# Attention and two expert layers on one core: weights split in small pieces, four more tiles turned on TensorE, scatters of one expert unordered, surplus count moved ahead

## The chip, the cores and the metric

The kernel runs on one core of one Trainium2 chip. The time is the device time of one execution in microseconds (us); what counts is the median of the runs. Engines are named as in the profile: PE is TensorE's matmuls, PEld its weight loads, DVE VectorE, ACT ScalarE, POOL GpSimd, SP SyncE, which here issues DMAs.

## The reference

Three layers follow each other, on 4 x 768 = 3072 tokens of 384 numbers:

```
for t: state = alpha_t * state + k_t v_t^T ; y_t = q_t state        # 8 heads of 48
P = exp(x @ w_gate), 8 rounds of row and column scaling            # layer 1
out = sum_e P[:, e] * (relu(x @ w1[e]) @ w2[e])                    # all 8 experts, F = 1024
logits = x @ w_gate + log1p(exp(x @ w_noise)) * noise              # layer 2
top2 of logits, softmax weights of the two
out[rows of e] += weight * (relu(x[rows of e] @ w1[e]) @ w2[e])    # for each of 8 experts
```

All inputs and the output are float32.

## The kernel before

Every product of two float32 operands is made of three matmuls of 16-bit halves: hi x hi, hi x lo, lo x hi. So weights and activations are split into a hi and a lo half, a step that takes an ACT instruction (hi) and a DVE instruction (lo = value - hi).

**Weights.** An expert x (0 to 7 in layer 1, 8 to 15 in layer 2) has seven blocks: three row blocks of W1, 1024 wide, and four of W2. `w_load` brings one block from SP's queue into a staging tile `wst`, of which there are two. `w_split` makes its halves in `WT[x % 2]` with L145 on ACT and L147 on DVE, 1024 elements to an instruction for W1, 768 for W2. Experts 1 to 6 (`STR`) use a scheme of seven block products in place of eight; for them `w_sums` (L128 to L130, POOL) adds three combinations of W2's blocks, and the split of a W2 block is one of 192 and one of 1152.

**Layer 1.** For each expert and 512 tokens, `s1` makes four pairs of hidden blocks: 18 matmuls (L273) into two banks, evicted by ACT (L279, L280, L285, L291), DVE (L296, six instructions) and POOL (L292). Then `s2` (L307) makes the second product into long banks that DVE adds to acc with the weight P (L317). Expert 0, expert 7 and the end use the plain form `g1`/`g2` (L195, L199, L226, L236 to L244).

**Layer 2.** A gate and a routing chain (ACT and DVE, L713 to L803) find each token's two experts. It reads tokens turned by SP (`xf`, L696) from x, which L688 on ACT and L689 on DVE write; SP writes x out to `xd` (L690). Each expert has 832 slots, seven tiles of 128 (the last 64), done in units of tiles 0 to 2 and 3 to 6. L813, L817 and the index matmul L824 find the slots' tokens; `gather` (L851, POOL) fetches a slot tile's rows; `xpose` turns it through `turn`, by a DMA transpose on SP (L696), or on PE with an ACT copy (L700, L701) for expert 0's first three tiles. `g1b` is the first product (L867, evicted by L870 on ACT and L871 on DVE), `g2b` the second (L226, L879 on DVE); L880 on POOL adds its rows to the output by an indirect DMA, a scatter. Behind everything `overflow` counts slots that found no place, from L893 to L906, reads the count into a register (L918) and runs a loop over them (L919), which with these inputs has no round.

**Order.** All instructions stand in each queue as the program emits them. Matmul functions call `pump(t)`, which moves an emission clock by an estimate of PE's time and lets side chains emit what is due. `w_pump` takes a step of the weight queue at most every 6.0 units of that clock, or 2.2 once all of layer 1's experts have their place; a step loads block i, sums block i-1 and splits block i-2. `w_need` takes all remaining steps when an expert is about to be used. The framework adds waits between instructions that touch the same memory; two scatters into the output count as such.

## Time and profile before

| | us |
|---|---|
| median of 3 runs | 2074.77 |
| lowest, highest | 2073.38, 2074.82 |
| the profiled execution | 2075.67 |
| its span, first to last instruction | 2073.9 |
| PE busy in it | 1984.0 |
| DVE, ACT, POOL busy | 1228.6, 671.5, 622.2 |

The profile is one execution taken by the hardware profiler; its times count from the first instruction. A timeline row gives the start, the length, the engine, the line, the operation with the tile written and the tiles read, the shape, and in brackets how long the engine idled before it and what released it. Rows of like instructions in a row are joined ("x3"). The names are those of the program's tiles: bank and long are accumulators of PE, wst the staging tile of weights, wt the split weights, hid the hidden activations, acc the sums of layer 1 and later slot tiles, ss the block sums.

### The profile page before, as it was taken

What the parts mean: (1) busy time and instruction counts of PE and PEld (TensorE: products, weight loads), DVE (VectorE), ACT (ScalarE), POOL (GpSimd) and SP (SyncE); (2) the same over time, 40 slices, a digit from 0 to 9 for tenths busy, and PEclk for the clock granted to TensorE, in tenths of its full rate; (3) what the DMA queues carried; (4) which work ended last, traced back from release to release, by engine and by line L of the source; (5) the groups of instructions that cost most, each with busy time, mean ns of one, the idle gap of its engine ahead of it and who ended that gap; (6) DMA issues with size and microseconds to landing.
All of it is one profiled execution on the core that took longest, in us unless ns stands there. A gap on an engine that the chain in (4) does not pass through costs nothing. (4 is left out here: it accounts for less than half of the span.)

```text
span 2073.9 us, 37502 instructions
## 1 busy us (share of the span) xinstructions
PE 1984.0 (96%) x15667; PEld 1332.4 (64%) x15667; DVE 1228.6 (59%) x2513; ACT 671.5 (32%) x1201; POOL 622.2 (30%) x452
## 2 busy tenths in 40 slices
PE   6999999999999999999999999999999889999996
PEld 5887656667667766776776677666555545555553
DVE  8889675765675576567557556554336645445431
ACT  5554422422342243234224323332222313222220
POOL 2433212422342352234225222321001234333322
PEclk9999999999999999999999999999999989999998
DMA  6333010100010010001001001003423448656631
GB/s 214 98 109 103 21 41 21 41 21 1 19 44 1 1 42 21 1 26 37 1 1 52 11 1 42 1 1 95 133 69 81 111 84 187 112 128 123 132 78 24
DMA packets 119580, 121.06 MB, mean 58 GB/s; under 512 B 68708, under 2 KB 101757, under 8 KB 119408
## 3 DMA queue, kind: packets, MB, share of 16 engines
q1 hardware_dynamic: 107984, 99.22, 17.2%
q0 software_dynamic: 11136, 18.89, 5.4%
q8 instruction: 124, 2.03, 0.4%
q10 hardware_dynamic: 288, 0.52, 0.1%
q14 instruction: 48, 0.39, 0.1%
HBM read 85.17 MB, written 21.63 MB: 51 GB/s over the span
## 5 line engine op out<-in xcount | busy, mean ns | idle before, releaser
L273 PE MATMUL bank<-xh,wt 128*128 128x512 f16 x1728 | 522.0, 380 | 6.3 <-DVE ss L296 3.8
L307 PE MATMUL long<-wt,hid 128*128 128x192 f16 x6048 | 508.8, 246 | 14.2 <-DVE acc L317 9.2
L292 POOL TENSOR_TENSOR hid<-ss,hid 128x1024 f16<-128x1024 f32 x144 | 307.0, 2132 | 705.6 <-ACT hid L291 651.3
L307 PEld LDWEIGHTS <-hid 128*128 128x128 f16 x6048 | 499.6, 98 | 27.1 <-issue 11.1
L273 PEld LDWEIGHTS <-wt 128*128 128x128 f16 x2592 | 253.1, 98 | 306.3 <-PE bank L273 6.1
L226 PE MATMUL bank<-wt,hid 128*128 128x384 f16 (+1 forms) x2496 | 422.4, 326 | 1.3 <-DVE hid L871 1.3
L226 PEld LDWEIGHTS <-hid 128*128 128x128 f16 (+1 forms) x2496 | 243.6, 99 | 162.6 <-issue 2.5
L273 PE MATMUL bank<-xl,wt 128*128 128x512 f16 x864 | 328.1, 380 | 0.0
L317 DVE SCALAR_TENSOR_TENSOR acc<-long,Pm,acc 128x192 f32<-128x192 f32 (+1 forms) x360 | 187.4, 534 | 169.8 <-PE long L307 167.5
L296 DVE SCALAR_TENSOR_TENSOR ss<-bank,ss 128x256 f32<-128x256 f32 x576 | 241.7, 421 | 58.2 <-ACT hid L285 39.6
L296 DVE SCALAR_TENSOR_TENSOR hid<-bank,hid 128x256 f16<-128x256 f32 (+1 forms) x288 | 159.1, 552 | 180.6 <-ACT ss L280 180.6
L291 ACT ACTIVATE hid<-ss 128x1024 f16<-128x1024 f32 x144 | 152.2, 1057 | 241.2 <-DVE ss L296 241.2
L147 DVE SCALAR_TENSOR_TENSOR wt<-wst,wt 128x1024 f16<-128x1024 f32 (+3 forms) x129 | 167.6, 1312 | 50.7 <-ACT wt L145 50.2
L867 PEld LDWEIGHTS <-wt 128*128 128x128 f16 x1152 | 112.3, 98 | 103.3 <-DMA xh<-acc 12.8
L279 ACT ACTIVATE hid<-bank 128x256 f16<-128x256 f32 x144 | 53.3, 370 | 382.9 <-PE bank L273 382.9
L880 POOL DMA_INDIRECT out_dram<-acc,ix x56 | 88.5, 1579 | 267.4 <-DVE acc L879 161.9
L870 ACT ACTIVATE hid<-bank 128x384 f16<-128x384 f32 (+1 forms) x128 | 65.4, 516 | 257.2 <-PE bank L867 255.9
L145 ACT ACTIVATE wt<-wst 128x1024 f16<-128x1024 f32 (+3 forms) x129 | 111.2, 882 | 94.9 <-DMA wst<-in_moe_w_dram 71.0
L871 DVE SCALAR_TENSOR_TENSOR hid<-bank,hid 128x384 f16<-128x384 f32 (+1 forms) x128 | 74.5, 589 | 106.0 <-ACT hid L870 106.0
L195 PE MATMUL bank<-xh,wt 128*128 128x512 f16 x384 | 121.8, 379 | 0.7 <-DVE acc L317 0.7
L867 PE MATMUL bank<-xh,wt 128*128 128x384 f16 (+1 forms) x576 | 107.6, 345 | 12.4 <-DMA xh<-acc 12.4
L285 ACT ACTIVATE hid<-bank 128x512 f16<-128x512 f32 x144 | 86.0, 597 | 66.3 <-PE bank L273 66.3
(187 smaller groups left out, 1655.1 us busy)
## 6 DMA issues: line engine op xcount, KB each, us to landing
wst<-in_moe_w_dram SPq DMA_DIRECT2D x45, 512.0 KB, 3.4
wst<-in_moe_w_dram SPq DMA_DIRECT2D x60, 384.0 KB, 3.2
la<-in_alpha_dram SPq DMA_DIRECT2D x24, 260.0 KB, 2.8
lk<-in_k_dram SPq DMA_DIRECT2D x24, 256.0 KB, 3.0
wt<-in_q_dram SPq DMA_DIRECT2D x22, 256.0 KB, 3.9
out_dram<-zero SPq DMA_DIRECT2D x6, 768.0 KB, 4.4
xd<-x SPq DMA_DIRECT2D x24, 192.0 KB, 1.9
wt<-in_v_dram SPq DMA_DIRECT2D x16, 192.0 KB, 4.1
```

What stands on the lines that cost most here:

```text
L145: nc.scalar.activation(t[:, o:o + n], src, AF.Copy, scale=SW)
L147: nc.vector.scalar_tensor_tensor(t[:, o + o1:o + o1 + n], src, SW, t[:, o:o + n], op0=OP.mult, op1=OP.subtract)
L195: nc.tensor.matmul(p, w1s(e, a, kc, f), x[:, kc, s], start=(n == 0), stop=(n == 3 * KC - 1))
L226: nc.tensor.matmul(p, h(a, f, s), w2s(x, b, f), start=(f + n == 0), stop=(f == FC - 1 and n == 2))
L273: nc.tensor.matmul(p, w1s(e, a, kc, f), x[:, kc, tok], start=(n == 0), stop=(n == 3 * KC - 1))
L291: nc.scalar.activation(lefts(e, nb, j, 0, S1, 4), sums, AF.Copy)
L292: nc.gpsimd.tensor_sub(lefts(e, nb, j, 1, S1, 4), sums, lefts(e, nb, j, 0, S1, 4))
L296: nc.vector.scalar_tensor_tensor(out, p, 0.0, x, op0=OP.max, op1=op)
L307: nc.tensor.matmul(out, left(e, nb, j, a, aop)[:, q * 128:(q + 1) * 128], w2t(e, b, wop, j), start=start and n == 0, stop=stop and n == 3 ...
L317: nc.vector.scalar_tensor_tensor(a, p, Pm[:, T, e:e + 1], a, op0=OP.mult, op1=OP.add)
L867: nc.tensor.matmul(p, w1s(x, a, kc, f), xt[:, b * KC + kc, :], start=(i == 0), stop=(i == 3 * KC - 1))
L880: nc.gpsimd.indirect_dma_start(out=out, out_offset=bass.IndirectOffsetOnAxis(ap=ix, axis=0), in_=y, in_offset=None, bounds_check=N - 1, oo ...
```

## The change

Four edits. First, `w_split`'s work is cut into pieces of at most 512 elements (W1) or 384 (W2), and `w_queue` becomes a generator: a step issues the hi of one piece and the lo of the piece before, with the next block's load at a block's first piece and the next block's `w_sums` at its third. The first step loads two blocks and issues the first hi at once. An expert of `STR` has 22 pieces, another 14, where there were 11 and 7. The spacing is 5.0 units for experts 2 to 6 and 2.2 for the others. Second, all seven slot tiles of expert 0 are turned on PE. Third, scatters of one expert are declared independent of each other; those of different experts still wait. Fourth, what `overflow` computed ahead of its read is emitted at unit 6 of layer 2, and only the read and the loop stay at the end.

```diff
--- before.py
+++ after.py
@@ -129,23 +129,35 @@
         g.tensor_sub(c[6], c[4], c[3])
         g.tensor_add(c[7], c[2], c[6])
 
-    def w_split(x, i, st):
-        t = W[x]
+    def w_pieces(x, i, st, most=1024):
+
         if i < KC:
-            todo = [(st[:, :F], i * F, F)]
+            todo = [(0, i * F, F)]
             o1 = W1N
         elif x in STR:
             o = 2 * W1N + (i - KC) * 7 * ND
-            todo = [(st[:, :ND], o, ND), (st[:, 2 * ND:8 * ND], o + ND, 6 * ND)]
+            todo = [(0, o, ND), (2 * ND, o + ND, 6 * ND)]
             o1 = W2N
         else:
-            todo = [(st[:, :2 * DM], 2 * W1N + (i - KC) * 2 * DM, 2 * DM)]
+            todo = [(0, 2 * W1N + (i - KC) * 2 * DM, 2 * DM)]
             o1 = FC * DM
-        for src, o, n in todo:
-            nc.scalar.activation(t[:, o:o + n], src, AF.Copy, scale=SW)
-        for src, o, n in todo:
-            nc.vector.scalar_tensor_tensor(t[:, o + o1:o + o1 + n], src, SW, t[:, o:o + n], op0=OP.mult,
-                                           op1=OP.subtract)
+        for c, o, n in todo:
+            m = n // -(-n // most)
+            for d in range(0, n, m):
+                yield st[:, c + d:c + d + m], W[x][:, o + d:o + d + m], W[x][:, o + o1 + d:o + o1 + d + m]
+
+    def w_hi(src, hi, lo):
+        nc.scalar.activation(hi, src, AF.Copy, scale=SW)
+
+    def w_lo(src, hi, lo):
+        nc.vector.scalar_tensor_tensor(lo, src, SW, hi, op0=OP.mult, op1=OP.subtract)
+
+    def w_split(x, i, st):
+        p = list(w_pieces(x, i, st))
+        for a in p:
+            w_hi(*a)
+        for a in p:
+            w_lo(*a)
 
     def w_alloc(x):
         W[x] = WT[x % 2]
@@ -844,6 +856,7 @@
 
     rng = {"r": 0, "y": 0}
     RW = {}
+    SC = {}
 
     def gather(e, j):
         r = M2["rows"][rng["r"] % len(M2["rows"])]
@@ -854,7 +867,7 @@
         RW[e, j] = r
 
     def xpose(e, j, dst):
-        turn(dst, RW.pop((e, j)), e == 0 and j < J0)
+        turn(dst, RW.pop((e, j)), e == 0)
 
     def g1b(x, par, f, xt, n):
         if f == 0:
@@ -877,11 +890,18 @@
         y = M2["ys"][rng["y"] % len(M2["ys"])][:n]
         rng["y"] += 1
         nc.vector.tensor_scalar(y, p, wc, None, op0=OP.mult)
-        nc.gpsimd.indirect_dma_start(out=out, out_offset=bass.IndirectOffsetOnAxis(ap=ix, axis=0), in_=y,
-                                     in_offset=None, bounds_check=N - 1, oob_is_err=False, compute_op=OP.add)
-
-
-    def overflow():
+        d = nc.gpsimd.indirect_dma_start(out=out, out_offset=bass.IndirectOffsetOnAxis(ap=ix, axis=0), in_=y,
+                                         in_offset=None, bounds_check=N - 1, oob_is_err=False, compute_op=OP.add)
+        if x < 2 * E:
+
+            for o in SC.setdefault(x, []):
+                tc.declare_no_dep(d.ins, o, reason="rows of one expert's slots are distinct")
+            SC[x].append(d.ins)
+
+
+    OV = {}
+
+    def overflow_count():
         V = nc.vector
         so = ctx.enter_context(tc.tile_pool(name="over", bufs=1))
 
@@ -915,6 +935,12 @@
         vs, vt = t("vs", [128, NT, 5], BF), t("vt", [128, E, NT, 5], BF)
         ri1, ri2 = t("ri1", [128, KC], I32), t("ri2", [128, FC], I32)
         xto = t("xto", [128, 2 * KC, 128], F16)
+        OV.update({k: v for k, v in locals().items() if k not in ("V",)})
+
+    def overflow():
+        V = nc.vector
+        t, tot, NO, it, sel, s2, eb, rb, cu, ce, ei, w1i, w2i, vs, vt, ri1, ri2, xto = [
+            OV[k] for k in "t tot NO it sel s2 eb rb cu ce ei w1i w2i vs vt ri1 ri2 xto".split()]
         nv = nc.values_load(tot[0:1, 0:1], min_val=0, max_val=E * NO)
         with tc.For_i(0, nv, 1):
             V.tensor_scalar(sel, ce, it, None, op0=OP.is_le)
@@ -969,7 +995,6 @@
 
     NB = N // 512
     NW = KC + 4
-    st_ = {}
     ws0 = [0]
 
     def w0_step():
@@ -1098,28 +1123,47 @@
     queued = set()
 
     def w_queue(x):
-        wq.append(lambda: w_alloc(x))
-        for i in range(NW + 2):
-            def f(i=i):
-                if i > 1:
-                    w_split(x, i - 2, st_.pop((x, i - 2)))
-                if 0 < i <= NW:
-                    w_sums(x, i - 1, st_[x, i - 1])
-                if i < NW:
-                    st_[x, i] = w_load(x, i)
-            wq.append(f)
+
+        def steps():
+            w_alloc(x)
+            st = [w_load(x, 0), w_load(x, 1)]
+            last = None
+            for i in range(NW):
+                p = list(w_pieces(x, i, st[i], 512 if i < KC else 384))
+                if x in STR and i == KC:
+                    w_sums(x, i, st[i])
+                    yield
+                for n, a in enumerate(p):
+                    w_hi(*a)
+                    if last is not None:
+                        w_lo(*last)
+                    if n == 0 and i and i + 1 < NW:
+                        st.append(w_load(x, i + 1))
+                    if n == 2:
+                        w_sums(x, i + 1, st[i + 1]) if i + 1 < NW else None
+                    last = a
+                    yield
+            w_lo(*last)
+
+        s = steps()
+
+        def step():
+            return next(s, 0) is None
+
+        wq.append(step)
 
     w_at = [0.0]
 
     def w_pump():
         if wq and clk[0] >= w_at[0]:
-            wq.pop(0)()
-            w_at[0] = clk[0] + (6.0 if len(W) < E else 2.2)
-
+            if not wq[0]():
+                wq.pop(0)
+            w_at[0] = clk[0] + (5.0 if 2 < len(W) < E else 2.2)
 
     def w_need(x):
         while x not in W or (wq and x == max(W)):
-            wq.pop(0)()
+            if not wq[0]():
+                wq.pop(0)
 
     def gates(Ts):
         c = []
@@ -1243,6 +1287,8 @@
         if m < len(order2):
             e, j0, j1 = order2[m]
             a = [(lambda f=f: u1(m, f), 9 * ((min(CAP, j1 * 128) - j0 * 128) / 2400.0 + 0.0025)) for f in range(FC)]
+            if m == 6:
+                chain([(overflow_count, 1.0)])
             if m >= 4 and j0 == 0:
                 chain(columns(e, J0, NJ) + (rows_in(e + 1, 0, NJ, NT, NJ) + columns(e + 1, 0, J0) if e + 1 < E else []))
         if m:
```

Where the order moves, first on DVE, in layer 1, at the end of a cycle of expert 2 while expert 3's weights are split. Before (L296 evicts s1's banks, L317 those of s2):

```order
L296 SCALAR_TENSOR_TENSOR hid<-bank,hid 128x256
L296 SCALAR_TENSOR_TENSOR ss<-bank,ss 128x256
L147 SCALAR_TENSOR_TENSOR wt_3694<-wst,wt_3694 128x192
L147 SCALAR_TENSOR_TENSOR wt_3694<-wst,wt_3694 128x1152
L296 SCALAR_TENSOR_TENSOR ss<-bank,ss 128x256 x3
L296 SCALAR_TENSOR_TENSOR hid<-bank,hid 128x512
L317 SCALAR_TENSOR_TENSOR acc<-long,Pm,acc 128x192
L317 SCALAR_TENSOR_TENSOR acc<-long,Pm,acc 128x384
L317 SCALAR_TENSOR_TENSOR acc<-long,Pm,acc 128x192
```

After (L153 is now the lo, L308 and L329 are what L296 and L317 were):

```order
L308 SCALAR_TENSOR_TENSOR hid<-bank,hid 128x512
L153 SCALAR_TENSOR_TENSOR wt_3694<-wst,wt_3694 128x512
L308 SCALAR_TENSOR_TENSOR hid<-bank,hid 128x256
L308 SCALAR_TENSOR_TENSOR ss<-bank,ss 128x256 x4
L308 SCALAR_TENSOR_TENSOR hid<-bank,hid 128x512
L308 SCALAR_TENSOR_TENSOR hid<-bank,hid 128x256
L308 SCALAR_TENSOR_TENSOR ss<-bank,ss 128x256
L153 SCALAR_TENSOR_TENSOR wt_3694<-wst,wt_3694 128x512
L308 SCALAR_TENSOR_TENSOR ss<-bank,ss 128x256 x3
L308 SCALAR_TENSOR_TENSOR hid<-bank,hid 128x512
L329 SCALAR_TENSOR_TENSOR acc<-long,Pm,acc 128x192
```

The pairs of 192 and 1152 elements are gone; single pieces stand between the evictions.

Next on ACT, at the flush ahead of expert 1 of layer 2, behind the routing's exponentials. Before (L145 is the hi, L760 the routing, L870 g1b's eviction):

```order
L145 ACTIVATE wt_3694<-wst 128x1024
L145 ACTIVATE wt_3694<-wst 128x768
L760 ACT_TABLE_LOAD
L760 ACTIVATE wb<-wb 128x10
L145 ACTIVATE wt_3694<-wst 128x768 x3
L870 ACTIVATE hid<-bank 128x384 x8
L870 ACTIVATE hid<-bank 128x448 x14
```

After (L150 is the hi, L772 the routing, L883 g1b's eviction, L713 the copy of a tile turned on PE):

```order
L150 ACTIVATE wt_3694<-wst 128x512
L150 ACTIVATE wt_3694<-wst 128x384
L772 ACT_TABLE_LOAD
L772 ACTIVATE wb<-wb 128x10
L150 ACTIVATE wt_3694<-wst 128x384 x7
L883 ACTIVATE hid<-bank 128x384 x8
L713 ACTIVATE xh<-bank 128x6x128 x3
L713 ACTIVATE xh<-bank 128x6x64
L883 ACTIVATE hid<-bank 128x448 x8
```

The five hi instructions of 1024 and 768 elements have become nine of 512 and 384, with the same evictions behind them, and four copies of turned tiles have come between the two units' evictions.

Last on POOL, the end of its queue, with the semaphores that an instruction waits for in brackets (DMASW are those of POOL's own DMAs). Before:

```order
L880 DMA out_dram<-acc,ix 3072x384 [waits DMASW4_49,DVE_49]
L880 DMA out_dram<-acc,ix 3072x384 [waits DMASW5_49,DVE_49]
L880 DMA out_dram<-acc,ix 3072x384 [waits DMASW6_49,DVE_49]
L893 IOTA oth 128x22
L908 IOTA ei 128x8
L910 IOTA w1i 128x3
L912 IOTA w2i 128x8
L918 TENSOR_LOAD tot [waits DVE_49]
```

After:

```order
L893 DMA out_dram<-acc,ix 3072x384 [waits DMASW4_49,DMASW5_49,DMASW3_49,DMASW6_49,DMASW2_49,DMASW7_49,DMASW0_49,DVE_49]
L893 DMA out_dram<-acc,ix 3072x384 [waits DVE_49] x6
L944 TENSOR_LOAD tot [waits DVE_49]
```

The last six scatters wait for DVE alone, only an expert's first waits for those before it, and nothing but the read stands behind them.

## Rows read from the trace of the kernel before

**Rows 1.** The page: busy time by engine; a load's issue to landing.

```profile
PE 1984.0 (96%) x15667; PEld 1332.4 (64%) x15667; DVE 1228.6 (59%) x2513; ACT 671.5 (32%) x1201; POOL 622.2 (30%) x452
...
wst<-in_moe_w_dram SPq DMA_DIRECT2D x45, 512.0 KB, 3.4
```

**Rows 2.** Timeline of weight loads in layer 1: starts of s2.

```profile
376.67 3.04 PEld L307 LDWEIGHTS <-hid 128*128 128x128 f16 x35
...
442.31 7.74 PEld L307 LDWEIGHTS <-hid 128*128 128x128 f16 x92
...
530.51 14.01 PEld L307 LDWEIGHTS <-hid 128*128 128x128 f16 x168
...
559.91 3.04 PEld L307 LDWEIGHTS <-hid 128*128 128x128 f16 x35
...
622.19 7.90 PEld L307 LDWEIGHTS <-hid 128*128 128x128 f16 x94
...
1279.50 2.05 PEld L307 LDWEIGHTS <-hid 128*128 128x128 f16 x23
...
1310.78 14.01 PEld L307 LDWEIGHTS <-hid 128*128 128x128 f16 x168
```

**Rows 3.** Timeline, expert 3's weights: DVE's pair, PE's two waits.

```profile
593.48 3.24 DVE L147 SCALAR_TENSOR_TENSOR wt<-wst,wt 128x192 f16<-128x192 f32 x2
...
594.50 3.23 PE L307 MATMUL long<-wt,hid 128*128 128x192 f16 x37 [0.41 <-POOL hid L292]
598.95 6.26 PE L307 MATMUL long<-wt,hid 128*128 128x192 f16 x74 [1.23 <-DVE acc L317]
```

**Rows 4.** Timeline of PE: three single waits.

```profile
310.78 0.38 PE L273 MATMUL bank<-xh,wt 128*128 128x512 f16 x1 [2.54 <-DVE acc L236]
...
1445.69 0.19 PE L713 MATMUL bank<-g,xf 128*128 128x32 f16 x1 [2.42 <-DMA xf<-x]
...
1733.66 0.76 PE L824 MATMUL bank<-rhs,acc 128*128 128x35 bf16 x24 [2.24 <-DVE rhs L817]
```

**Rows 5.** Timeline of SP, ACT and PE, first unit of layer 2.

```profile
1604.42 1.22 SPq L112 DMA_DIRECT2D wst<-in_moe_w_dram  x1
...
1606.31 0.49 ACT L870 ACTIVATE hid<-bank 128x384 f16<-128x384 f32 x1 [3.25 <-PE bank L867]
...
1616.94 0.19 PE L713 MATMUL bank<-g,xf 128*128 128x32 f16 x1 [1.59 <-DMA xf<-x]
```

**Rows 6.** Timeline of POOL, SP and PE: expert 0's tiles 3 to 6.

```profile
1655.56 1.56 POOL L880 DMA_INDIRECT out_dram<-acc,ix  x1 [3.84 <-issue]
...
1661.46 0.99 POOL L851 DMA_INDIRECT acc<-xd,ix  x1 [0.30 <-issue]
...
1660.94 5.68 SPq L696 DMA_TRANSPOSE xh<-acc  x4
...
1668.72 2.77 PE L867 MATMUL bank<-xh,wt 128*128 128x448 f16 x7 [12.43 <-DMA xh<-acc]
```

**Rows 7.** Timeline of DVE and POOL, the end.

```profile
2053.84 0.61 DVE L879 TENSOR_SCALAR acc<-bank,wc 64x384 f32<-64x384 f32 x1 [3.40 <-PE bank L226]
...
2060.05 1.42 POOL L880 DMA_INDIRECT out_dram<-acc,ix  x1 [3.40 <-DMA out_dram<-acc,ix]
...
2062.74 0.13 DVE L904 CAST tot<-cu 1x1 int32<-1x1 f32 x1
```

**Rows 8.** Timeline of DVE: lo halves while little else runs.

```profile
296.73 0.35 DVE L147 SCALAR_TENSOR_TENSOR wt<-wst,wt 128x192 f16<-128x192 f32 x1
297.42 1.36 DVE L147 SCALAR_TENSOR_TENSOR wt<-wst,wt 128x1152 f16<-128x1152 f32 x1 [0.35 <-ACT wt L145]
```

**Rows 9.** Timeline of ACT and DVE: flush ahead of layer 2's expert 1.

```profile
1634.17 0.84 ACT L145 ACTIVATE wt<-wst 128x768 f16<-128x768 f32 x1 [3.19 <-DMA wst<-in_moe_w_dram]
...
1635.16 0.95 DVE L147 SCALAR_TENSOR_TENSOR wt<-wst,wt 128x768 f16<-128x768 f32 x1
```

**Rows 10.** Busy time by window: PE, PEld, DVE, ACT, POOL; granted clock, DMA.

```profile
1734.00:2053.80 319.80, 319.80 (x1985) 186.59 (x1981) 143.35 (x311) 79.83 (x132) 102.26 (x77) 1.00 0.56 111
```

## The prediction

> **What bounds the kernel now.** I read the page's busy times first: PE works 96% of the span, DVE 59%, ACT 32%, POOL 30% [rows 1]. So time can be won only where PE stands still, or in what follows PE's last instruction, and work put on DVE, ACT or POOL costs nothing as long as PE does not wait for it. From there I followed PE's idle time in the timeline, stretch by stretch, and looked for what released each wait. Three kinds came out.
>
> First, in layer 1, PE alternates between s1 (L273) and s2 (L307) in cycles that can be measured from one s2 to the next, on the weight-load rows. An undisturbed cycle runs from 530.51 to 559.91: 29.40 us. While expert 3's weights are split, two cycles take 559.91 to 622.19, 62.28, which is 3.48 more than two undisturbed ones; experts 4, 5 and 6 repeat that pattern (four times 3.48 = 13.9). Expert 2's two cycles, 376.67 to 442.31, lose 65.64 - 58.80 = 6.84, and expert 7's one, 1279.50 to 1310.78, loses 1.88. Together **22.6 us** go in cycles in which weights are split [rows 2]. Why is seen on DVE: a pair of lo halves (192 and 1152 elements) holds it 3.24 us in one piece at 593.48, the evictions of s1's banks and s2's banks stand behind it, and PE then waits 0.41 for POOL's part of hid and 1.23 for DVE's acc [rows 3].
>
> Second, five single waits at the seams: 2.54 at the change of bank pools, 2.42 for a transposed token tile, 2.24 for the right-hand side of the index matmul [rows 4], and in the first experts of layer 2 one of 1.59 [rows 5] and one of 12.43 [rows 6].
>
> Third, the end: DVE evicts the last tile at 2053.84, but the last scatter is issued only at 2060.05, since each waits for the landing of the one before; the count of surplus slots comes after it, and its last result stands at 2062.74. From its end, 2062.87, to the span's end at 2073.9 lie 11.0 us of leaving the loop [rows 1, 7].
>
> **The change part by part.** The profiled execution took 2075.67 us; the sum is made against it. The median of three runs, 2074.77, is 0.9 lower, and I take that off at the end.
>
> *Small pieces in layer 1.* A lo piece has at most 512 elements and stands alone between two groups of evictions. Quiet rows give its price: 192 elements took 0.35, 1152 took 1.36 [rows 8], so 1.05 ns an element and 0.15 fixed, and 512 take 0.69. The pair at 593.48 took 3.24 where the quiet prices make 1.71, a factor of 1.9 [rows 3, 8], so a piece beside POOL's work takes up to 1.3. PE's two waits behind the pair come to 1.64, so that DVE could be held for 3.24 - 1.64 = 1.6 without harm [rows 3]; 1.3 is less. The steps of one expert are also spread wider: 23 at 5.0 units of the emission clock instead of 9 at 6.0. What may stay is POOL: w_sums is as long as before and still stands ahead of L292 in some blocks; one wait of 0.41 for it [rows 3] at each of five sums for some of the experts makes 2 to 4, of which I take 3. **-19.6**; bounds -13 (a third of the losses stays) and -22 (nearly all goes).
>
> *Expert 1 and the seam at 310.* Expert 1's splits now come more often, and early, so less of them stands in front of L236 at the pool change. A shorter DVE queue takes part of the 2.54 [rows 4], I take somewhat over half: **-1.5**, between 0 and -2.5.
>
> *The token tile at 1445.* Its transpose stands on SP's queue behind a weight load that waits for a staging buffer. With the lo of a smaller, earlier piece as the last reader, this buffer comes free sooner: **-2.0** of 2.42 [rows 4], between 0 and -2.4.
>
> *First experts of layer 2, three terms.* (a) The first hi piece is now issued on ACT right behind its own load. SP issues that load at 1604.42, and a 512 KB load takes 3.4 us to land [rows 1, 5], so ACT is blocked until about 1608.6, where it evicted at 1606.31 before. Queued behind are the first g1b evictions and the L688 copies, on which the xd writes and the xf transposes on SP depend, past a load that now waits for a lo piece of its own. PE's wait for xf, 1.59 [rows 5], grows by 2.3 plus half a microsecond of pieces: **+3.0** (2 to 4). (b) In the flush ahead of expert 1 the last weight load now waits for a lo piece that stands behind the routing chain r4 on DVE. Before, its hi started at 1634.17 and its lo at 1635.16, with r4 ahead of that; now a lo of 0.55, and then a landing of up to 3.4, follow on 1635.16, so that DVE's evictions behind all this start near 1639.1 instead of 1636.1: **+3.1** (0 to 4) [rows 1, 9]. (c) After its last g2b matmul PE waits 12.43 for expert 0's four slot tiles. POOL's scatter at 1655.56 waits 3.84 for the one before, the gathers stand behind it, and SP's four transposes start at 1660.94 with 5.68 us of issue [rows 6]. The fourth gather is issued at 1661.46; with a landing taken as long as a load's, 3.4, its tile is there at 1664.9, and six PE transposes and one ACT copy of 768 elements, as long as the 0.84 of another ACT row of 768, end near 1666.2 instead of PE's 1668.72: -2.5, without SP's row of four [rows 1, 6, 9]. And the scatter ahead need not wait, which brings the gathers forward by half of the 3.84, -1.9; the other half goes to DVE's eviction, which then sets this scatter. **-4.4** (-2 to -7). Together **+1.7**, bounds -5 and +6.
>
> *The index matmul at 1733.* Its right-hand side stood on DVE behind a lo that waited for a load. Fewer pieces now stand ahead: **-2.2** of 2.24 [rows 4], between 0 and -2.2.
>
> *The rest of layer 2.* From 1734 to 2053.8 PE is busy 319.80 of 319.80 us [rows 10]: here the change can only lose. Seven more pieces an expert cost DVE 7 x 0.15 = 1 us, hidden as it idles over half of the stretch. The blocking first hi costs ACT a landing, 3.4, behind the flush's last one, say 7 us in all. PE's cover is the banks: 319.80/1985 is 0.161 a matmul, nine matmuls fill a bank in 1.45, eight banks hold 11.6 us. **0**, up to +3.
>
> *The end.* The scatters of the last expert no longer wait for each other, so the last one follows DVE's 2053.84 + 0.61 at about 2054.8 instead of 2060.05, and no count follows: the read of the count starts near 2056.2 instead of 2062.9, and the 11.0 us behind stay [rows 7]. **-6.6**; -5 if the landing of the last scatter, which the exit waits for, comes after that, -7.5 at best.
>
> **Sum:** 2075.67 - 19.6 - 1.5 - 2.0 + 1.7 - 2.2 + 0 - 6.6 = 2045.5; less 0.9, 2044.6: **2045 us**.
>
> **The rivals.** *Pieces that still collide.* If each small piece meets POOL, half of layer 1's gain goes: of the 22 pieces for each of experts 2 to 6, 110 in all, a fifth that make PE wait 0.4 to 0.5, as it did for POOL's hid [rows 3], come to 10: 2055 us. For it: the pair's factor of 1.9; against: a piece leaves DVE free again behind it. Chance 0.16. [...]
>
> *Fixed cost of more instructions.* 11 more pieces for each of six experts cost DVE 66 x 0.15 = 9.9 us; were DVE the path there, the time would be 2055. DVE's 59% speaks against. Chance 0.05. [...] The trace shows 0.15 for the fixed part, and PE does not wait for it.
>
> *The end stays.* If the exit is bound by the queue's drain and not by the scatters, or the declared independence leaves the waits in place, the 6.6 stay: 2052. The instruction order shows these waits gone; the count is moved for certain. Chance 0.09.
>
> *Slower.* ACT's blocked first piece and the flush ahead of each layer-2 expert: beyond 11.6 us of blocked ACT, PE stops. To turn the sum over, it takes some 5 us for each of seven experts, so blocks of 16.6 us, five landings of 3.4 in a row: 2045 + 35 = 2080. Against: the old flush already holds such a row of pieces, with PE never waiting [rows 10]. Chance 0.06.
>
> **How the numbers follow.** Forecast 0.64 (2038 to 2051), rivals 0.16, 0.05, 0.09 and 0.06. The range **2037 to 2056** takes in the bounds of the terms and the first three rivals' times, and leaves out the slow end and the far sides. About 4 us, 0.2%, is what can be told from no change. Faster 0.91, within 0.2% 0.03, slower 0.06.
>
> **What would show it.** Cycles of 29.4 between s2's in experts 2 to 7, with no DVE row over 1.4 us among L153; PE's wait for xf near 4.5 and the wait for xh near 8; at the end each scatter right behind its eviction, and 11 us of leaving behind the read of the count. It is wrong if the cycles still show 1 us or more each, if PE waits in 1734 to 2050, or if the wait for xh stays at 12.

## The result

The changed kernel takes **2049.76 us**, median of four runs (2048.4 to 2050.4); the kernel before, in the same runs, 2074.39 (2073.38 to 2074.82). The ratio is 0.9876, with a 95% interval from 0.9862 to 0.9889: 24.6 us, or 1.2%, faster. The forecast was 2045, in a range from 2037 to 2056; the time lies inside, 4.8 above the forecast.

The two profiled executions, 2075.67 and 2048.4, differ by 27.3, since that of before is above its median and that of the changed kernel is the fastest of its four. What follows is read from these two, so its sums come to 27.2, the difference of the spans.

The page of the changed kernel (span, then busy time by engine), which answers to [rows 1]:

```profile
span 2046.7 us, 37798 instructions
...
PE 1984.3 (97%) x15691; PEld 1334.8 (65%) x15691; DVE 1247.3 (61%) x2642; ACT 681.5 (33%) x1334; POOL 602.7 (29%) x452
```

PE's busy time, in which its stretches at half clock (a granted clock of 0.50 or 0.51 in windows below) count too, is the same to 0.3 us. On balance, what was won is time in which PE stood still (21.2 us) or had ended (6.3); stretches at half clock went in some places and came in others.

Where s2 starts in layer 1, timeline of weight loads, while expert 3's weights are split; it answers to [rows 2]:

```profile
553.05 14.01 PEld L319 LDWEIGHTS <-hid 128*128 128x128 f16 x168
...
582.45 14.01 PEld L319 LDWEIGHTS <-hid 128*128 128x128 f16 x168
...
611.85 14.01 PEld L319 LDWEIGHTS <-hid 128*128 128x128 f16 x168
```

Twice 29.40, and one unbroken row of 168 loads in each: an undisturbed s2. All cycles of experts 3 to 6 read like this. Expert 2's lose 0.85, 0.52 and 1.16, expert 7's 1.80, where they lost 6.84 and 1.88.

PE's single waits, timeline, to be held against [rows 4 to 6]:

```profile
309.91 0.38 PE L285 MATMUL bank<-xh,wt 128*128 128x512 f16 x1 [1.63 <-DVE acc L248]
...
1597.25 0.21 PE L725 MATMUL bank<-g,xf 128*128 128x32 f16 x1 [4.48 <-DMA xf<-x]
1597.43 3.04 PE L880 MATMUL bank<-xh,wt 128*128 128x384 f16 x9
...
1628.48 0.66 PE L238 MATMUL bank<-wt,hid 128*128 128x384 f16 x3 [0.93 <-DVE hid L884]
1630.57 1.14 PE L238 MATMUL bank<-wt,hid 128*128 128x384 f16 x3 [1.43 <-DVE hid L884]
...
1646.83 0.51 PE L712 MATMUL bank<-i,acc 128*128 128x128 f16 x6 [2.57 <-DMA acc<-xd,ix]
...
1651.38 2.99 PE L880 MATMUL bank<-xh,wt 128*128 128x448 f16 x8 [0.64 <-ACT xh L713]
```

The waits for the token tile at 1445 and for the index matmul at 1733 have no row any more. The wait for xf has grown to 4.48, and the nine matmuls behind it take 3.04 where nine took 1.62 in the undisturbed piece ahead of it. The wait of 12.43 has become four short ones (2.57, 0.72, 0.39 and 0.64) with transposes between them. The end, timeline of DVE and POOL, answers to [rows 7]:

```profile
2032.97 0.61 DVE L892 TENSOR_SCALAR acc<-bank,wc 64x384 f32<-64x384 f32 x1 [3.40 <-PE bank L238]
...
2029.85 1.55 POOL L893 DMA_INDIRECT out_dram<-acc,ix  x1 [2.35 <-DVE acc L892]
2033.86 1.42 POOL L893 DMA_INDIRECT out_dram<-acc,ix  x1 [2.46 <-DVEq L945]
```

The last scatter stands 0.9 behind DVE's eviction instead of 6.2.

Cut at the same PE instructions, the two traces differ like this (before, after; starts of the named matmuls, in us):

| stretch | before | after | difference |
|---|---|---|---|
| up to the first s1 | 310.78 | 309.91 | -0.9 |
| layer 1's cycles of s1 and s2 | 1084.32 | 1064.25 | -20.1 |
| up to layer 2's first g1b | 209.55 | 207.91 | -1.6 |
| to the first matmul behind the wait for xf and its gate | 12.45 | 15.36 | +2.9 |
| to the second unit's g1b | 13.38 | 15.98 | +2.6 |
| to the end of g2b ahead of tiles 3 to 6 | 25.81 | 30.85 | +5.0 |
| to the g1b of tiles 3 to 6 | 12.43 | 7.12 | -5.3 |
| that unit and its g2b, to expert 1's second unit | 32.58 | 31.35 | -1.2 |
| to expert 2's first unit | 32.96 | 30.66 | -2.3 |
| from there to PE's last instruction | 319.54 | 319.54 | 0.0 |
| behind PE's last instruction | 20.06 | 13.74 | -6.3 |

### The profile page after: what moved, and what is told of

The parts are those of the page before. It is cut to its first block, busy times and chain, and to the rows that moved or that the text cites. A ratio compares the mean times of both kernels' runs of the same rounds, so it can differ in the third digit from the quotient of the medians.

```text
span 2046.7 us, 37798 instructions
## 1 busy us (share of the span) xinstructions
PE 1984.3 (97%) x15691; PEld 1334.8 (65%) x15691; DVE 1247.3 (61%) x2642; ACT 681.5 (33%) x1334; POOL 602.7 (29%) x452
## 5 line engine op out<-in xcount | busy, mean ns | idle before, releaser
L304 POOL TENSOR_TENSOR hid<-ss,hid 128x1024 f16<-128x1024 f32 x144 | 306.7, 2130 | 701.8 <-ACT hid L303 658.7
L329 DVE SCALAR_TENSOR_TENSOR acc<-long,Pm,acc 128x192 f32<-128x192 f32 (+1 forms) x360 | 187.5, 534 | 148.1 <-PE long L319 147.4
L308 DVE SCALAR_TENSOR_TENSOR hid<-bank,hid 128x256 f16<-128x256 f32 (+1 forms) x288 | 159.3, 553 | 185.8 <-ACT ss L292 185.8
L308 DVE SCALAR_TENSOR_TENSOR ss<-bank,ss 128x256 f32<-128x256 f32 x576 | 241.0, 421 | 48.0 <-ACT hid L297 31.2
L303 ACT ACTIVATE hid<-ss 128x1024 f16<-128x1024 f32 x144 | 152.2, 1057 | 231.8 <-DVE ss L308 231.8
L153 DVE SCALAR_TENSOR_TENSOR wt<-wst,wt 128x384 f16<-128x384 f32 (+2 forms) x258 | 200.8, 789 | 23.6 <-ACT wt L150 23.6
L291 ACT ACTIVATE hid<-bank 128x256 f16<-128x256 f32 x144 | 53.2, 369 | 409.1 <-PE bank L285 409.1
L150 ACT ACTIVATE wt<-wst 128x384 f16<-128x384 f32 (+2 forms) x258 | 132.1, 538 | 130.9 <-DMA wst<-in_moe_w_dram 130.7
L883 ACT ACTIVATE hid<-bank 128x384 f16<-128x384 f32 (+1 forms) x128 | 63.7, 515 | 167.0 <-PE bank L880 167.0
L880 PE MATMUL bank<-xl,wt 128*128 128x384 f16 (+1 forms) x576 | 105.3, 339 | 0.0
```

The costliest lines, as they stand in the source:

```text
L150: nc.scalar.activation(hi, src, AF.Copy, scale=SW)
L153: nc.vector.scalar_tensor_tensor(lo, src, SW, hi, op0=OP.mult, op1=OP.subtract)
L303: nc.scalar.activation(lefts(e, nb, j, 0, S1, 4), sums, AF.Copy)
L304: nc.gpsimd.tensor_sub(lefts(e, nb, j, 1, S1, 4), sums, lefts(e, nb, j, 0, S1, 4))
L308: nc.vector.scalar_tensor_tensor(out, p, 0.0, x, op0=OP.max, op1=op)
L329: nc.vector.scalar_tensor_tensor(a, p, Pm[:, T, e:e + 1], a, op0=OP.mult, op1=OP.add)
```

## Which edit gives what: each one alone

Four kernels hold one edit each. First the pieces:

```diff
-        turn(dst, RW.pop((e, j)), e == 0)
+        turn(dst, RW.pop((e, j)), e == 0 and j < J0)
-            for o in SC.setdefault(x, []):
-                tc.declare_no_dep(d.ins, o, ...)
...
-            if m == 6:
-                chain([(overflow_count, 1.0)])
...
+    overflow_count()
     overflow()
```

> The small pieces alone, with the slot tiles, the scatters and the count as before. Theory (PE's waits add up, stretch by stretch, and a short wait that makes the granted clock fall costs its slow matmuls too): as in the changed kernel, layer 1's cycles give 18.4 us, the seam at 310 2.6, the token tile at 1445 2.2 and the index matmul at 1733 2.2; the first experts of layer 2 lose 5.5 at PE's wait for xf (2.9 longer, 2.6 in matmuls at half clock) and 5 at the flush; the wait for expert 0's tiles stays near 12.4 and the end stays at 20 us behind PE. Sum about -15: 2059. Rival (the pieces carry the whole result, the three other edits nothing): 2050.

Measured: 2059.99 in four runs, ratio 0.9924 (0.9907 to 0.9941), so 15.2 less than the 2075.21 of its own runs of before, as summed. The cycles lose what they lose in the changed kernel, the first matmul behind the wait for xf comes late in the same way, and 19.7 us stand behind PE's last instruction. One row missed: the wait for xh is 10.45, where 12.4 was expected. The pieces do not carry the rest.

Then the turns on PE:

```diff
-        turn(dst, RW.pop((e, j)), e == 0 and j < J0)
+        turn(dst, RW.pop((e, j)), e == 0)
```

> The kernel before, with expert 0's tiles 3 to 6 turned on PE, nothing else. Theory: the four transposes leave SP, PE's wait for xh falls from 12.4 to about 10, its matmuls at half clock behind the wait stay; about -2.5: 2072. Rival (the gathers alone set that wait): the wait stays at 12 or more and the time within 1 us of before.

Measured: 2069.52 in one run; PE ends 5.55 earlier than in the trace of before. That is twice the expectation. The g1b of tiles 3 to 6 starts 3.5 earlier, and then the unit behind it takes 31.05 instead of 32.58. The timeline of PE and the windows (busy PE, PEld, DVE, ACT, POOL, then granted clock, DMA share, GB/s) show why:

```profile
1660.71 0.82 PE L700 MATMUL bank<-i,acc 128*128 128x128 f16 x6 [4.63 <-DMA acc<-xd,ix]
1661.94 0.82 PE L700 MATMUL bank<-i,acc 128*128 128x128 f16 x6 [0.41 <-DMA acc<-xd,ix]
1663.11 1.46 PE L700 MATMUL bank<-i,acc 128*128 128x128 f16 x12 [0.35 <-DMA acc<-xd,ix]
1665.21 13.08 PE L867 MATMUL bank<-xh,wt 128*128 128x448 f16 x63 [0.64 <-ACT xh L701]
```

```profile
1660.00:1666.00 6.00, 3.89 (x27) 2.76 (x28) 0.00 (x0) 2.81 (x4) 3.54 (x3) 0.54 0.46 92
1666.00:1669.00 3.00, 3.00 (x14) 1.40 (x13) 0.30 (x1) 0.54 (x1) 0.00 (x0) 0.79 0.07 12
1668.70:1674.00 5.30, 5.30 (x30) 2.74 (x29) 5.30 (x26) 1.63 (x3) 0.00 (x0) 1.00 0.01 3
```

In the trace of before the granted clock was 0.51 from 1668.7 to 1674, in matmuls of 448 columns:

```profile
1668.70:1674.00 5.30, 5.28 (x15) 2.19 (x16) 1.15 (x5) 0.55 (x1) 0.00 (x0) 0.51 0.00 0
```

Here part of the stretch at half clock passes while the short transposes run, and the matmuls are back at 1.00 from 1668.7 on. What this is worth is not sharp: the same unit took 31.57 with the pieces alone, without these transposes, and 31.35 with them in the changed kernel.

Then the scatters:

```diff
+            for o in SC.setdefault(x, []):
+                tc.declare_no_dep(d.ins, o, reason="rows of one expert's slots are distinct")
+            SC[x].append(d.ins)
```

> The kernel before, with scatters of one expert not ordered among each other, nothing else. Theory: the scatter ahead of expert 0's gathers goes out about 2 us sooner and PE's wait for xh falls from 12.4 to about 10.4; at the end the last scatter follows PE by 1 us instead of 6.3, the count still behind it, so 5.3 less: together -7, 2067. Rival (the exit is bound by the queue's landing and drain, not by the scatters' order): the end stays at 20 us behind PE, and only 2 are gained, 2072.

Measured: 2071.71 in ten runs, ratio 0.9979 (0.9969 to 0.9988): 3.5, half of what was expected. The two mechanisms are there in the profile, at their size: PE's wait for xh is 10.27, 2.2 shorter, and 14.7 us stand behind PE's last instruction, 5.3 less.

```profile
1668.09 12.19 PE L868 MATMUL bank<-xh,wt 128*128 128x448 f16 x54 [10.27 <-DMA xh<-acc]
```

```profile
2055.88 1.42 POOL L881 DMA_INDIRECT out_dram<-acc,ix  x1 [2.46 <-DVE acc L880]
```

1.2 goes back at once: the wait for the index matmul's right-hand side grows from 2.24 to 3.47, since PE gets there sooner and DVE does not. Another 1.2 goes behind that longer wait, where the matmuls run at a granted clock of 0.65 (1733.5 to 1738); in the trace of before it is 1.00 behind the wait of 2.24. The profiled execution also reached its first s1 1.9 later than that of before, ahead of everything that was changed (below).

Last the count:

```diff
+            if m == 6:
+                chain([(overflow_count, 1.0)])
```

> The kernel before, with the count of surplus slots emitted at unit 6 of layer 2, nothing else. Theory: the scatters are still in a row, the last one issued 6.2 us behind PE and landed 9 us behind it; the exit waits for that landing anyway, so the count's 2.9 us behind the scatter are worth at most 1.4: 2073 to 2074. Rival (the count is what sets the end): 2.9 gained or more, 2071.

Measured: 2073.88 in one run, 18.6 behind PE's last instruction, 1.5 less. From the end of the last scatter's instruction to the end of the span lie 12.39 in the four traces with the count behind it (before, the pieces, the turns, the scatters) and 11.3 to 11.4 without, so the count is worth about 1. That the exit waits for the scatter's landing, as expected, is not shown. One run, where before spreads from 2072.3 to 2080.4, shows no gain by its time. With both edits it is 13.7, so the scatters' order was most of the end.

## Size or density of the pieces

The prediction held that the length of one piece decides: 1.3 fits where 3.2 did not. Four kernels vary the length and the density of the steps. Large pieces, spread:

```diff
-                p = list(w_pieces(x, i, st[i], 512 if i < KC else 384))
+                p = list(w_pieces(x, i, st[i], 1024 if i < KC else 1152))
-                    if n == 2:
+                    if i >= KC and n == min(2, len(p) - 1):
-            w_at[0] = clk[0] + (5.0 if 2 < len(W) < E else 2.2)
+            w_at[0] = clk[0] + (10.0 if 2 < len(W) < E else 4.4 if len(W) <= E else 2.2)
```

> The changed kernel with pieces as large as before (1024; 192 and 1152; 768), the steps spread over as many cycles as in the changed kernel (10.0 units for experts 2 to 6, 4.4 for 1, 7 and 8). Theory (the length of one DVE instruction decides): pairs of 3.2 us between evictions still stop PE, layer 1's cycles lose 3 or more for each of experts 3 to 6 and some 15 to 22 in all. Rival (the spread decides, not the size): experts 3 to 6 lose less than 1 each, and layer 1 about 4 to 6 in all, as the changed kernel does.

Small pieces, dense:

```diff
-            w_at[0] = clk[0] + (5.0 if 2 < len(W) < E else 2.2)
+            w_at[0] = clk[0] + (2.6 if 2 < len(W) < E else 2.2)
```

> The changed kernel with its small pieces, issued twice as densely for experts 2 to 6 (2.6 units), so that an expert's weights take as many cycles as before. Theory (the length of one DVE instruction decides): experts 3 to 6 lose less than 1 each, layer 1 at most 10. Rival (the spread decides): they lose 2 to 3.5 each again, layer 1 some 15 to 20.

The kernel before, with its steps wider and nothing else:

```diff
-            w_at[0] = clk[0] + (6.0 if len(W) < E else 2.2)
+            w_at[0] = clk[0] + (12.0 if 2 < len(W) < E else 6.0 if len(W) < E else 2.2)
```

> The kernel before with one number changed: steps 12.0 units of the emission clock apart for experts 2 to 6, not 6.0; the pieces as large as they were, the pair of 192 and 1152 still in one step. Theory now (how much DVE and POOL work falls into one cycle decides, more than the length of a piece): layer 1's cycles lose 8 or less instead of 24.6 (1.9 of it ahead of expert 7, which no weights cause), so some 15 below before, 2059. Rival (a pair of 3.2 stops PE wherever it stands): the same number of pairs costs the same, 3 or more for each of experts 3 to 6, and the time stays within 4 of before.

Large single pieces, dense, against the first of these:

```diff
-            w_at[0] = clk[0] + (10.0 if 2 < len(W) < E else 4.4 if len(W) <= E else 2.2)
+            w_at[0] = clk[0] + (5.0 if 2 < len(W) < E else 4.4 if len(W) <= E else 2.2)
```

> The kernel with large single pieces, its steps as dense as in the kernel before (5.0 units for experts 2 to 6 in place of 10.0): 192, 1152 and 1024 elements, but one in a step. It closes the square of size and density. Theory (density decides, size adds about 2): layer 1's cycles lose 22 to 26, as the dense small pieces (22.2) and the kernel before (24.7) do. Rival (cutting the pair of 192 and 1152 in two steps is what counts): they lose 12 or less.

What the 35 cycles from one s2 to the next lose against 29.40 each, summed over each trace (1.94 of every sum is the last cycle, ahead of expert 7, which no weights cause):

| kernel | DVE pieces in a step | steps an expert, spacing | lost, us | time, us |
|---|---|---|---|---|
| before | 192 and 1152 together | 9, 6.0 | 24.7 | 2074.4 |
| only spaced | 192 and 1152 together | 9, 12.0 | 28.3 | 2080.6 (10 runs) |
| small, dense | one, up to 512 | 23, 2.6 | 22.2 | 2065.3 (1 run) |
| large, dense | one, up to 1152 | 12, 5.0 | 9.0 | 2050.2 (1 run) |
| large, spread | one, up to 1152 | 12, 10.0 | 8.3 | 2049.1 (1 run) |
| changed kernel | one, up to 512 | 23, 5.0 | 6.3 | 2049.8 (4 runs) |

The times come from sets of runs in which before took 2074.1 to 2076.6, and they hold layer 2 as well, so it is the column of the lost time that compares.

The first two expectations said that size or spread decides, and on these I took the spread for the cause; the third kernel refuted that, with a ratio of 1.0016 (1.0005 to 1.0026), and its rival was nearer. In the fourth the theory (density decides) failed as well, and its rival came true. What fits all six kernels is **one piece in a step, with steps of 5 units or more**. Taking the pair apart goes with 15.6 of the 18.4 that were won, 1.0 of it ahead of expert 7, whose steps stand wider there; a wider spread of the large pieces 0.7, and smaller pieces on top 2.0. The two kernels with large pieces also space expert 7 wider, which is 0.9 of theirs, so size may be worth up to 3. In the large, dense kernel a piece of 3.15 at 558.32 costs its cycle 0.07, and one stretched to 2.15 at 589.59, where s2 begins to need its banks, lets PE's weight loads wait 0.85 (DVE's timeline, then PEld's):

```profile
558.32 3.15 DVE L153 SCALAR_TENSOR_TENSOR wt<-wst,wt 128x1152 f16<-128x1152 f32 x1
...
589.59 2.15 DVE L153 SCALAR_TENSOR_TENSOR wt<-wst,wt 128x192 f16<-128x192 f32 x1
```

```profile
583.11 8.15 PEld L319 LDWEIGHTS <-hid 128*128 128x128 f16 x97
592.12 5.87 PEld L319 LDWEIGHTS <-hid 128*128 128x128 f16 x71 [0.85 <-issue]
```

So no single slack fits, and the 1.6 that the prediction derived from one pair is not it: 3.15 fitted in one place and 2.15 did not in another. In the kernel with steps of 12.0 one of expert 3's four pairs, stretched to 4.21 beside POOL's L292 and w_sums, falls 3.8 us behind the start of an s2, and PE's weight loads wait 2.22 behind it (DVE, then PEld):

```profile
623.13 4.21 DVE L147 SCALAR_TENSOR_TENSOR wt<-wst,wt 128x192 f16<-128x192 f32 x2 [0.78 <-ACT wt L145]
...
627.72 7.85 PEld L307 LDWEIGHTS <-hid 128*128 128x128 f16 x95 [2.22 <-issue]
```

A pair at 607.51 in the same trace, in the midst of s1 and not beside L292, took 0.35 and 1.36 and nothing waited; one of 3.40 at 650.84, across the start of the next s2, cost its cycle 0.02. So the place of a piece counts too, and with one kernel for each mix of size and density the place is not held apart. With small pieces at 2.6 units there is a piece in nearly every s1 block, of 3.9 us. There a piece of 1.37 at 587.12 holds up DVE's evictions, ACT's L303 comes late behind them, then POOL's L304, and PE waits for it; w_sums had left POOL 0.22 before that L304 started, so it is not what PE waits for (POOL, then PEld):

```profile
590.91 2.13 POOL L304 TENSOR_TENSOR hid<-ss,hid 128x1024 f16<-128x1024 f32 x1 [0.22 <-ACT hid L303]
...
593.09 5.06 PEld L319 LDWEIGHTS <-hid 128*128 128x128 f16 x62 [0.77 <-POOL hid L304]
598.61 5.87 PEld L319 LDWEIGHTS <-hid 128*128 128x128 f16 x71 [0.45 <-issue]
```

The generator does more than cut the pair: it issues a lo one step behind its hi, and puts w_sums beside the lo of 192 or of one small piece, not beside both. Which of these brings the 15.6 was not separated; no kernel here does one without the others.

## What layer 1 still loses

```diff
-            w_at[0] = clk[0] + (5.0 if 2 < len(W) < E else 2.2)
+            w_at[0] = clk[0] + (7.0 if len(W) == 3 else 5.0 if 2 < len(W) <= E else 2.2)
```

> The changed kernel, steps 7.0 units apart for expert 2 and 5.0 for expert 7 instead of 5.0 and 2.2. Theory (too much DVE and POOL work in one cycle is what is left in layer 1): of the 2.5 that expert 2 still costs about 1 goes, of expert 7's 1.8 all: 2047. Rival (these losses have another source, expert 1's own extra DVE work and the last cycle): within 1 us of the changed kernel.

Measured: 2045.72 in one run. Layer 1 loses 4.0, of which 1.94 is the last cycle; expert 2 costs 2.0 instead of 2.5 and expert 7 0.1 instead of 1.8. For expert 7 density was the cause. For expert 2 it was so only in part. Layer 1 makes up 2.2 of the 4.0 between this run and the changed kernel's median; the rest was not traced.

## What the new queue costs at the start of layer 2

First, the hi pieces issued two steps later:

```diff
             last = None
+            if x >= E:
+                yield
+                yield
```

> The changed kernel, with the first hi of a layer-2 expert issued two steps of the weight queue behind its loads, nothing else. Theory (ACT, blocked on the load's landing, keeps the token tiles from SP, and the wait makes the clock fall): ACT evicts at once again, PE's wait for xf falls from 4.5 to about 1.6 or less and the matmuls behind it run at full clock, 5.5 gained; two more pieces fall into the flush, 0 to 3 lost there: 2045 to 2048. Rival (SP's queue, with the loads ahead of the turns, sets that wait): it stays near 4 and the time at 2050.

Measured: 2048.19 in one run, with PE's end 0.4 earlier than in the changed kernel. ACT evicts at once, as expected, and the wait for xf falls to 2.39, not to 1.6. The next stretch is 0.9 shorter. But the flush behind it (the steps that w_need issues at once when an expert is about to be used), now with more pieces, gives 2.0 of that back, and 0.9 more goes from expert 2 on. The mechanism is right and the mend is not.

Then the old queue, load, split of a whole block two steps later, for layer 2's expert 1 alone:

```diff
     def w_queue(x):
+        if x == E + 1:
+            return w_queue_old(x)
```

> The changed kernel with the old queue for layer 2's expert 1 alone. Theory: PE's wait for xf falls from 4.5 to 1.6, its matmuls behind it run at full clock again, and DVE's waits behind the flush fall from 3.6 to about 1.3: 5 to 9 less than the changed kernel by PE's end. Rival (both come from SP's order or from the turns on PE, not from the queue): under 2 less.

Measured: 2038.41 in one run, 11.4 below the changed kernel's median; from the first g1b of layer 2 to PE's end 10.8 less, more than the 5 to 9 expected. PE's timeline:

```profile
1594.73 1.62 PE L880 MATMUL bank<-xh,wt 128*128 128x384 f16 x9
1596.92 11.86 PE L238 MATMUL bank<-wt,hid 128*128 128x384 f16 x72
...
1620.39 4.18 PE L238 MATMUL bank<-wt,hid 128*128 128x384 f16 x23
1625.67 3.26 PE L238 MATMUL bank<-wt,hid 128*128 128x384 f16 x19 [1.10 <-DVE hid L884]
```

The nine matmuls take 1.62 again and the 72 behind them 11.86 instead of 13.03; the granted clock is 1.00 from 1594.7 to 1600, where it was 0.50 from 1597 to 1602 in the changed kernel. Behind the flush PE waits for DVE once, 1.10, instead of four times, 3.60, and the granted clock stays at 1.00 there, where in the changed kernel it fell:

```profile
1628.00:1634.00 6.00, 2.94 (x9) 0.78 (x9) 5.83 (x27) 0.00 (x0) 0.00 (x0) 0.68 0.01 3
1634.00:1637.00 3.00, 2.90 (x10) 1.38 (x11) 2.44 (x11) 0.00 (x0) 0.28 (x1) 0.50 0.00 0
```

So in this one place the new queue costs 11, twice what the turns on PE win. ACT's and DVE's rows of the changed kernel show both halves of it, the first hi that holds the evictions until 1586.91, and two loads of the flush that DVE's evictions wait for until 1622.59:

```profile
1586.37 0.63 ACT L150 ACTIVATE wt<-wst 128x512 f16<-128x512 f32 x1 [5.89 <-DMA wst<-in_moe_w_dram]
1586.91 0.47 ACT L883 ACTIVATE hid<-bank 128x384 f16<-128x384 f32 x1
...
1615.76 0.94 ACT L150 ACTIVATE wt<-wst 128x384 f16<-128x384 f32 x2 [3.47 <-DMA wst<-in_moe_w_dram]
1621.09 0.94 ACT L150 ACTIVATE wt<-wst 128x384 f16<-128x384 f32 x2 [4.39 <-DMA wst<-in_moe_w_dram]
```

```profile
1616.16 1.96 DVE L153 SCALAR_TENSOR_TENSOR wt<-wst,wt 128x384 f16<-128x384 f32 x4
1621.65 1.03 DVE L153 SCALAR_TENSOR_TENSOR wt<-wst,wt 128x384 f16<-128x384 f32 x2 [3.53 <-ACT wt L150]
1622.59 1.01 DVE L884 SCALAR_TENSOR_TENSOR hid<-bank,hid 128x384 f16<-128x384 f32 x2
```

The two kernels with large pieces show which part is whose. They too issue the first hi right behind its load, and PE's wait for xf is 6.55 (spread) and 5.79 (dense) there, longer than 4.48. But with 7 steps for that expert in place of 14, the last lo stands before the second unit, PE waits for no eviction behind the flush, and from the second unit's g1b to that of tiles 3 to 6 pass 30.93 and 31.16 instead of 37.97. So the blocked hi costs at xf, and the many small pieces cost at the flush.

Both edits together, the spacing and the old queue for that expert:

> The changed kernel with two edits: the weight steps 7.0 units apart for expert 2 and 5.0 for expert 7, and for layer 2's expert 1 alone the queue of the kernel before (load, then the split of a whole block two steps later). Theory (what layer 1 still loses comes from too dense steps; in layer 2 the changed queue costs a longer wait for xf, matmuls at half clock, and DVE's waits behind the flush): 3 to 4 from layer 1 and 5 to 9 from layer 2 below the changed kernel, 2037 to 2042. Rival (a wait ahead of expert 0's tiles only grows by what is gained before it, as the gathers set it): 3 to 5 below, 2045 to 2046.

Measured: **2035.17** in five runs (2034.09 to 2038.09), ratio to before 0.9797 (0.9782 to 0.9812): 14.6 below the changed kernel's median and some 40 below the kernel before. In the profile layer 1 gives 2.3, less than the 3 to 4 expected, and layer 2 gives 11.0, more than the 5 to 9.

## Why the prediction held, and where it was off

- **What bounds the kernel** held: PE's busy time did not move, and each microsecond won or lost has a wait, a stretch at half clock, or the exit behind it.
- **Small pieces in layer 1**, -19.6: the cycles gave -18.4. The size of the term was right, its reason was not. The step that failed is the slack of 1.6, against which a piece of 1.3 was held: single pieces of up to 3.15 cost 2 to 3 in all, and pieces of at most 512 set too densely cost nearly as much as before. The 1.3 failed too: L153 shows rows of 2.50 (at 527.57) and 2.35, over the 1.4 that was named as a sign, in cycles that lose nothing. The residue was not POOL's sums at each of experts 2 to 6, but experts 2 and 7, the latter from its spacing of 2.2, which the prediction passed over; with 1.16 and 1.80 two of these cycles show the 1 us or more that it gave as a sign of being wrong. The wait of 0.41 that it put down to those sums [rows 3] had another source: POOL had stood idle for 1.54 ahead of the L292 that PE waited for, until ACT's L291 ended.
- **The seam at 310**, -1.5: the wait fell by 0.9, and the matmuls behind it no longer run at half clock (0.66 from 311 to 316 before, 1.00 from 309.9 to 316 now), another 1.7. The second part was in no term, and in part it is luck: of the five traces with the old pieces, which wait 2.50 to 2.65 here, three have the half clock and two do not. The kernel with the count alone, the wait and then the clock:

```profile
311.13 0.38 PE L273 MATMUL bank<-xh,wt 128*128 128x512 f16 x1 [2.65 <-DVE acc L236]
```

```profile
311.10:316.10 5.00, 4.97 (x25) 2.47 (x26) 2.65 (x4) 1.73 (x4) 2.55 (x3) 1.00 0.38 120
```

- **The token tile**, -2.0: the stretch gives -1.6, as a wait of 0.39 for a gathered tile came in its place. **The index matmul**, -2.2: -2.3. Here smaller pieces are what counts, as forecast: both waits are gone or below 0.3 in all kernels with small pieces, and back in the two with large ones (1.72 and 2.28 for the token tile, 1.89 and 1.61 for the index matmul).
- **First experts of layer 2**, +1.7: (a) the wait for xf grew by 2.89 (+3.0 forecast; the working's 1608.6 does not follow from its rows, as 1604.42 and 3.4 make 1607.8), but half clock behind it added 2.6, which the sum left out although the row of 12.43 showed such a stretch. (b) +5.0 for +3.1: PE's waits grew by 2.3, by the mechanism told, with two landings in a row in the flush (3.47 and 4.39 on ACT) where the working had one; the other 2.7 are matmuls at half clock between and behind these waits (0.68 and 0.50, above), again in no term. (c) -5.3 for -4.4, and 1.2 more from the clock, by the transposes or by the run.
- **The rest of layer 2**, 0: 319.54 in both.
- **The end**, -6.6: -6.3. That the exit waits for the landing of the last scatter, as the bound of -5 has it, no run shows.
- **The offset**: sum and profile differ by 2.9 (2045.5 against 2048.4). The term that was mis-sized is that of the first experts, which measured +4.0 by the table, clock included, for +1.7; layer 1's pieces add 1.2, and the seam's clock gives 1.1 back. The median lies another 1.4 above that profile, and 0.9 had been taken off the sum, both inside the run-to-run spread below.
- **The rivals.** Neither the collision of pieces, nor the fixed cost, nor the end that stays came true. The fixed cost is there, 0.15 in the quiet rows [rows 8]. With 129 more pieces DVE's busy time rose by 18.7, but that is not a clean measure of it, since the large single pieces, dense, have as many instructions as before and 12.4 less. Larger pieces won nothing in layer 1: the kernels with pieces up to 1152 lose 2.0 and 2.7 more there than the changed kernel (8.3 and 9.0 against 6.3). The slower end found its place, ACT blocked on a landing (5.89), only in expert 1, where PE waits (4.48) for a token tile that ACT's copies feed and not for a bank, and not in the later ones. Pieces of 384 elements did take longer beside POOL: of the changed kernel's single rows between 320 and 1400, the 42 with POOL idle took 0.54 or 0.55, the 26 that overlap a POOL row 0.92 to 2.35. PE did not wait for the one at 587.77:

```profile
587.57 2.13 POOL L304 TENSOR_TENSOR hid<-ss,hid 128x1024 f16<-128x1024 f32 x1 [2.83 <-ACT hid L303]
...
587.77 2.35 DVE L153 SCALAR_TENSOR_TENSOR wt<-wst,wt 128x384 f16<-128x384 f32 x1
```

## What to carry to other kernels

Split side work so that one instruction stands alone between two evictions, and give it steps wide enough (5 units or more here); in layer 1 how long that instruction is (worth up to 3 us here) mattered less than whether a second one fell on the same spot (15.6 us), though the hi's and the sums' steps were moved in the same edit. A queue tuned for a stage that is full of matmuls can be wrong at a seam, as it was here by 11 us: ACT's first hi waited 5.89 for its DMA, the eviction behind it began only at 1586.91, and PE waited 4.48 for the token tile that ACT's copies feed. So look at each stage that shares the queue and let it keep its own order. Where PE must wait anyway, cost the slow matmuls behind the wait too (nine took 3.04 instead of 1.62 behind the wait of 4.48); small PE work at their front may take some of that on itself, which one kernel suggests (the turns alone, a granted clock of 0.54 from 1660 to 1666, with the transposes, and 1.00 from 1668.7) and none settles.

## What the hardware showed

- A lower granted clock (0.51 from 1668.7 to 1674 behind the wait of 12.43, in the trace of before) was also seen behind waits of a few microseconds, and there the length of the wait alone did not tell: behind 4.48 (changed kernel) it was 0.50 from 1597 to 1602, behind 2.54 at 310 (before) 0.66 to 316, behind 1.89 at 1711.9 (large, spread) 0.58 to 1716, and behind 2.39 at 1594 (late hi) nine matmuls took 2.47 instead of 1.62; behind 1.63 (changed kernel, at 309.9), 2.24 and 2.42 (before, at 1733 and 1445) and, in the kernel with the count alone, 2.65 it was 1.00.
- Some 2 to 3 us of the run-to-run spread arise before anything that was changed: the first s1 starts between 309.7 and 312.7 in the fourteen profiles, and from 20 to 50 us the granted clock was 1.00, 0.89 and 0.83 in the three windows below, of before, of the changed kernel and of the pieces alone. An effect of 1 or 2 us is to be read from a stretch of the trace, not from one time.

```profile
20.00:50.00 30.00, 23.73 (x343) 20.30 (x342) 29.27 (x47) 17.95 (x35) 7.40 (x8) 1.00 0.45 143
```

```profile
20.00:50.00 30.00, 22.54 (x334) 19.35 (x331) 28.95 (x47) 17.90 (x34) 8.07 (x8) 0.89 0.45 142
```

```profile
20.00:50.00 30.00, 24.61 (x308) 21.54 (x305) 26.42 (x42) 16.98 (x31) 6.93 (x8) 0.83 0.43 136
```
